# A decode step of two attention layers and two gated layers on one core: layer one's gated product, its turn and its products with w_down in two parts, in two PSUM banks, with another order of transfers

## The chip, the cores and the metric

The kernel runs on one core of one Trainium2 chip. The metric is the device time of one execution in microseconds; the figure for a kernel is the median of its runs. Three runs of the kernel before took 300.4, 301.22 and 302.75 us, so its time is 301.22 us. Lower is better.

## The reference, cut to what matters

```python
def _A_ref(x, k_cache, v_cache, wq, wo):        # x (4,1,512); caches (4,8,4096,128)
    q = (x @ wq).reshape(B, Sq, 32, 128).transpose(0, 2, 1, 3)
    k, v = repeat(k_cache, 4, axis=1), repeat(v_cache, 4, axis=1)
    p = softmax(einsum("bhqd,bhkd->bhqk", q, k) * 128 ** -0.5)
    o = einsum("bhqk,bhkd->bhqd", p, v)
    return o.transpose(0, 2, 1, 3).reshape(B, Sq, 4096) @ wo
def _B_ref(x, w_gate, w_up, w_down):            # 512 -> 1792 -> 512
    return (sigmoid(x @ w_gate) * (x @ w_up)) @ w_down
x = A_x
x = x + _A_ref(_layernorm(x), ...)              # attention, layer one
x = x + _B_ref(_layernorm(x), ...)              # gated layer, layer one
x = x + _A_ref(_layernorm(x), ...)              # attention, layer two: the same caches and weights
x = x + _B_ref(_layernorm(x), ...)
```

All arrays are bfloat16. The keys and the values of one sample are 8 heads of 4096 x 128 each, 8.4 MB; of four samples, keys and values together, 67 MB. Both attention layers read them, and a layer's result for a sample is needed before the next layer's query of that sample exists.

## The kernel before

**Units and tiles.** A unit is (sample b, half of the heads hg, layer l), written as three digits: 011 is sample 0, second half, layer two. There are sixteen; `UNITS` gives their order, and unit i of that order has the stages k{i}.0 and k{i}.1 (scores, L814), p{i} (softmax), v{i}.0 and v{i}.1 (products with the values, L942), o{i}.* (their sum turned and divided) and in layer one w{i}.* (products with wo, added to x). A tile is half of one head's keys or values, 128 x 2048 bfloat16, 0.52 MB. Keys are turned in place on VectorE before use (L824). The tiles of the second half of the heads (hg = 1) and one tile more stay in SBUF from layer one to layer two; those of the first half are loaded twice. So 114 MB are read.

**Transfers.** All of them are issued from SP's queue in the order of the string `LOADS`: `K2010` is the keys of unit 201, tiles 0 of a pair of heads, and makes two transfers of 0.52 MB; a last letter (`K201a`) makes one of 1.05 MB, both halves of a head. In this text transfers are numbered from 0 in this order; there are 156, in both kernels. A tile goes to a place in SBUF that the planner picks, and the issue waits until the last instruction that uses what was there is done. An issue that waits holds all behind it.

**Planner.** Every operation is put with a cost, a rank (with the shift that `SHIFTS` has for its stage) and what it reads and writes. `schedule` (L150) then plays the program through once, picks for each engine the operation that can start first (by rank among several), and so fixes the order on each engine, the places of the tiles, and fillers: matmuls on PE (L1329) with no use but to keep its clock up where it would idle. On the chip each engine runs its list in order.

**The chain of a sample.** When the last values of (b, 1, layer one) are in, `chain(b)` (L1127) runs: `layer_norm` (stage n), `gate_up` (g: 16 matmuls with w_gate into bank G, 16 with w_up into bank U, and on the way the norm's factor: PE, ACT, POOL), `gated` (h: tanh on ACT, L1092; product on VectorE, L1097; turn on VectorE, L1104), `down` (d: 56 matmuls with w_down, L1117, summed in bank G), the update of x (L1140), `layer_norm` again (m), and then the queries of layer two (q, L752). From then on the scores of unit (b, 1, 1) can be made, and the places that its kept keys hold come free. The chains of the four samples lie at about 87, 147, 198 and 253 us of the span. `gated` and `down` take a range of chunks of 128 rows of w_down (14 in all); the chain calls them once, with all 14. `last_chain` (L1212), the gated layer of layer two for all samples, calls `gated` in three parts already.

Of the kernel before, what the change touches and what calls it, by code (L numbers as in the profile page):

```python
# [7 lines left out]
ALU = mybir.AluOpType  # L8
# [31 lines left out]
class _Tile:  # L40
# [366 lines left out]
def bass_interleave_layers__gqa_block_cached__glu_gated_glu__decode_kernel(nc, A_x, A_k, A_v, A_wq, A_wo, B_x, B_wg, B_wu, B_wd, out):  # L407
    B, SQ, D = A_x.shape
    _, G, SK, DH = A_k.shape
# [4 lines left out]
    KD = D // P  # L414
# [7 lines left out]
    FB = FS // 32  # L422
# [6 lines left out]
    MORE = 64  # L429
# [3 lines left out]
    S = _Plan([SLOTS, 2, 2, 2, 2, 3, 3, 3, 8])  # L433
# [40 lines left out]
    q1 = sb("q1", [P, G, R, B], bf)  # L474
# [36 lines left out]
    G_ps = ps("G_ps", [P, 512])  # L511
    U_ps = ps("U_ps", [P, 512])
# [20 lines left out]
    def const(name, flat, first, parts):  # L533
# [15 lines left out]
        reads=["mask"], writes=["mask"], cost=0.3,  # L549
# [123 lines left out]
    def rank_v(u, pr):  # L673
# [9 lines left out]
        reads=["xin", "ident"], writes=[own("M", True)], cost=0.2, lock="M",  # L683
# [3 lines left out]
        reads=[own("M")], writes=[f"x{b}" for b in range(B)], cost=0.2, free="M",  # L687
# [391 lines left out]
    def gated(rs, rs_key, chunks, nb, rank, ends):  # L1079

        c0, c1 = chunks
        cols = slice(32 * c0, 32 * c1)
        share = (c1 - c0) / FB

        def dealt(t):
            return t[:, 0:FS].rearrange("p (i x) -> p i x", i=32)[:, :, c0:c1]

        def packed(t):
            return t[:, cols].rearrange("p (i x) -> p i x", i=32)

        S.put(
            "act", lambda e: e.activation(packed(th), dealt(G_ps), ACTF.Tanh, scale=rs),  # L1092
            reads=["G", rs_key] + [own("P") + "t0"] * (c0 > 0), writes=[own("P", c0 == 0) + f"t{c0}"], cost=0.18 + 0.47 * share, rank=rank, lock="P" if c0 == 0 else None,
        )
        S.put(
            "dve",
            lambda e: e.scalar_tensor_tensor(  # L1097
                out=packed(b1), in0=packed(th), scalar=1.0, in1=dealt(U_ps), op0=ALU.add, op1=ALU.mult,
            ),
            reads=[own("P") + f"t{c0}", "U"] + [own("B1") + "t0"] * (c0 > 0), writes=[own("B1", c0 == 0) + f"t{c0}"], cost=0.16 + 0.47 * share, rank=rank,  # L1100
            lock="B1" if c0 == 0 else None,
        )
        S.put(
            "dve", lambda e: e.transpose(  # L1104
                pt_h[:, cols].bitcast(dt.int32).rearrange("p (c i) -> p c i", i=32),
                b1[:, cols].bitcast(dt.int32).rearrange("p (i c) -> p c i", i=32),
            ),
            reads=[own("B1") + f"t{c0}"], writes=[own("P") + f"d{c0}"], cost=0.13 + 0.24 * share, rank=rank, free="B1" if c1 == FB else None,
        )

    def down(chunks, nb, o_ps, bank, rank):
        c0, c1 = chunks
        for k in range(KD):
            fns = []
            for c in range(c0, c1):
                rows = pt_h[:, 64 * (c // 2):64 * (c // 2) + 64].rearrange("p (i r) -> p i r", r=2)[:, 0:nb, c % 2]
                fns.append(lambda e, k=k, c=c, rows=rows: e.matmul(  # L1117
                    o_ps[:, k * MORE:(k + 1) * MORE], lhsT=wd[:, c, k * P:(k + 1) * P],
                    rhs=rows.unsqueeze(2).broadcast_to([P, nb, MORE // nb]),
                    start=(c == c0), stop=(c == c1 - 1),  # L1120
                ))
# [250 lines left out]
```

## Time and profile before

| | us |
|---|---|
| median of three runs | 301.22 |
| the profiled execution, whole | 301.75 |
| its span, first to last instruction | 300.0 |
| PE busy | 213.7 |
| VectorE (DVE) busy | 171.5 |
| ACT busy | 61.0 |
| share of the 16 DMA engines that q1's packets took | 94.8% |

The span has 1.75 us around it in this execution. A busy share is an average over the span; the engines wait for transfers at many places, and the transfers for places in SBUF at some. A row of the view by windows gives the busy time of each engine in a stretch, then the clock that PE was granted (1.00 is full), the share of the DMA engines in use and the rate of the transfers. In the chain of waits a row gives start, length, and the engine and line (or the transfer) that the end waited for at that time.

### The profile page before, as it was taken

Reading aid. Unit: us, or ns where it says so; the run is one execution under the profiler, and the core shown is the slowest. Engines: PE = TensorE matmul, PEld = TensorE weight load, DVE = VectorE, ACT = ScalarE, POOL = GpSimd, SP = SyncE. Lnnn points to the kernel's source line nnn. Section 1 sums busy time; section 2 is a strip of 40 time slices with the busy share of each in tenths; the row PEclk is TensorE's granted clock in tenths of the full one; section 3 lists DMA queues with packets and bytes.
Section 4 is the critical chain, followed back from the end, with each engine's and each line's share of the span. In section 5 each row is a group of like instructions: output and inputs, shape, how many; then the busy total and the mean of one; then the engine's idle time right before and its main releaser. Section 6 shows DMA issues by size and latency. Waiting matters only on the chain.

```text
span 300.0 us, 8879 instructions
## 1 busy us (share of the span) xinstructions
PE 213.7 (71%) x3977; PEld 129.4 (43%) x3977; DVE 171.5 (57%) x327; ACT 61.0 (20%) x155; POOL 13.0 (4%) x48
## 2 busy tenths in 40 slices
PE   1200205487888979688889878798886889898785
PEld 1200201134456637245456464456554355554462
DVE  4069593972004998956126986315997783258223
ACT  1100000123102210042323202322220233224212
POOL 8200000000000000000000000000000000000000
PEclk9999999559999999999999999999999799999999
DMA  6999999999999999999999999978999998999940
GB/s 263 384 412 413 419 411 424 414 422 417 401 416 407 376 415 419 417 417 412 407 407 354 406 413 413 411 304 352 354 416 423 417 407 323 398 401 417 416 178 4
DMA packets 25638, 114.62 MB, mean 382 GB/s; under 512 B 2560, under 2 KB 2560, under 8 KB 19840
## 3 DMA queue, kind: packets, MB, share of 16 engines
q1 hardware_dynamic: 25552, 114.04, 94.8%
q8 instruction: 31, 0.51, 0.7%
q14 instruction: 7, 0.06, 0.0%
q10 hardware_dynamic: 48, 0.01, 0.0%
HBM read 114.04 MB, written 0.00 MB: 380 GB/s over the span
## 4 chain that ended last, share of the span: by engine, by line
DMA 48%; PE 26%; SPq 14%; DVE 5%; issue 3%; ACT 2%; POOL 0%; DVEq 0%; ACTq 0%
DMA slots<-in_A_v_cache_dram 28%; DMA slots<-in_A_k_cache_dram 16%; SPq L603 13%; DMA wo<-in_A_wo_dram 5%; PE O_ps L962 4%; PE S_ps L832 4%; PE Q_ps L752 3%; PE M_ps L1003 3%; DVE slots L824 2%; PE G_ps L1117 2%; PE PT_ps L1329 2%; SPq L611 2%; PE M_ps L981 1%; ACT b L974 1%; PE G_ps L1065 1%
## 5 line engine op out<-in xcount | busy, mean ns | idle before, releaser
L824 DVE STREAM_TRANSPOSE slots<-slots 128x1024 int32<-128x1024 int32 x89 | 107.1, 1226 | 23.0 <-DMA slots<-in_A_k_cache_dram 21.5
L1329 PE MATMUL PT_ps<-even 128*128 128x256 bf16 x404 | 56.4, 273 | 0.8 <-ACT pt_sb L889 0.8
L832 PE MATMUL S_ps<-slots,qz 128*32 128x512 bf16 x488 | 39.7, 431 | 23.8 <-DVE slots L824 21.7
L962 PE MATMUL O_ps<-slots,pt_sb 128*16 128x512 bf16 x472 | 35.3, 381 | 12.5 <-DMA slots<-in_A_v_cache_dram 9.0
L1329 PEld LDWEIGHTS PT_ps<-even 128*128 128x128 bf16 x404 | 34.9, 99 | 15.8 <-issue 10.2
L974 ACT ACTIVATE b<-O_ps 128x512 bf16<-128x512 f32 x31 | 18.5, 595 | 59.8 <-PE O_ps L962 50.6
L832 PEld LDWEIGHTS S_ps<-slots,qz 128*32 128x32 bf16 x488 | 12.4, 100 | 41.2 <-DVE slots L824 25.3
L989 DVE TENSOR_TENSOR oT<-M_ps,rl 128x8 bf16<-128x8 f32 x31 | 4.7, 153 | 27.4 <-PE M_ps L981 27.4
L1003 PE MATMUL M_ps<-oT,wo 128*128 128x64 bf16 x512 | 19.0, 193 | 1.5 <-DVE x L1015 0.3
L962 PEld LDWEIGHTS O_ps<-slots,pt_sb 128*16 128x16 bf16 x472 | 9.6, 87 | 22.8 <-issue 7.1
L1003 PEld LDWEIGHTS M_ps<-oT,wo 128*128 128x128 bf16 x512 | 16.9, 98 | 6.0 <-DVE oT L989 2.4
L721 PE MATMUL Q_ps<-small,wq 128*128 128x4 bf16 x128 | 3.7, 166 | 21.3 <-DVE wsum L1306 18.8
L868 ACT ACTIVATE pp<-S_ps,tr 128x512 bf16<-128x512 f32 x16 | 13.3, 832 | 21.1 <-DVE tr L861 20.3
L981 PE MATMUL M_ps<-sel_o,b 128*64 128x64 bf16 x496 | 13.8, 199 | 4.4 <-ACT b L974 3.6
L981 PEld LDWEIGHTS M_ps<-sel_o,b 128*64 128x64 bf16 x496 | 10.4, 112 | 13.4 <-ACT b L974 10.5
L854 DVE TENSOR_REDUCE stat<-S_ps 128x1 f32<-128x512 f32 x16 | 10.9, 682 | 8.8 <-PE S_ps L832 8.7
L1055 POOL TENSOR_TENSOR stat<-stat 128x1 f32<-128x1 f32 x8 | 4.4, 551 | 251.5 <-ACT stat L1051 251.5
L889 ACT ACTIVATE pt_sb<-PT_ps 128x512 bf16<-128x512 f32 x16 | 9.5, 595 | 21.8 <-PE PT_ps L879 20.4
L801 DVE TENSOR_TENSOR qz<-Q_ps,maskrs 128x256 bf16<-128x256 f32 x16 | 6.5, 404 | 12.1 <-PE Q_ps L791 7.0
L721 PEld LDWEIGHTS Q_ps<-small,wq 128*128 128x128 bf16 x128 | 3.6, 104 | 21.5 <-DVE sq L1297 18.9
L796 ACT ACTIVATE maskrs<-mask,stat 128x16 f32<-128x16 f32 x16 | 4.5, 303 | 36.3 <-DVE qz L801 26.4
L1015 DVE SCALAR_TENSOR_TENSOR x<-M_ps,x 128x4 f32<-128x4 f32 x16 | 2.4, 148 | 12.6 <-PE M_ps L1003 12.4
(155 smaller groups left out, 205.1 us busy)
## 6 DMA issues: line engine op xcount, KB each, us to landing
slots<-in_A_v_cache_dram SPq DMA_DIRECT2D x51, 512.0 KB, 9.9
slots<-in_A_k_cache_dram SPq DMA_DIRECT2D x49, 512.0 KB, 7.7
slots<-in_A_k_cache_dram SPq DMA_DIRECT2D x20, 1024.0 KB, 13.1
slots<-in_A_v_cache_dram SPq DMA_DIRECT2D x19, 1024.0 KB, 13.7
wq<-in_A_wq_dram SPq DMA_DIRECT2D x2, 2048.0 KB, 15.0
wo<-in_A_wo_dram SPq DMA_DIRECT2D x4, 1024.0 KB, 13.6
wg<-in_B_w_gate_dram SPq DMA_DIRECT2D x1, 1792.0 KB, 26.5
wu<-in_B_w_up_dram SPq DMA_DIRECT2D x1, 1792.0 KB, 17.8
```

The lines of the kernel that those rows point to most:

```text
L603: return e.dma_start((ring if len(ts) == 1 else double)[ts[0].slot], src)
L752: fns.append(lambda e, c=c, k=k: e.matmul(Q_ps[:, c * WIDE:c * WIDE + MORE - c // 15 * WIDE], lhsT=wq[:, hg, k, c * DH:(c + 1) * DH], rhs= ...
L824: "dve", lambda e, t=t: e.transpose(ring[t.slot].bitcast(dt.int32), ring[t.slot].bitcast(dt.int32)),
L832: fns.append(lambda e, s=s, t=t, nn=nn, q=q: e.matmul(S_ps[qi][32 * s:32 * s + 32, :], lhsT=window(qi, s * NQ + nn, q), rhs=ring[t.slot].r ...
L854: dve(lambda e: e.tensor_reduce(ml[at], bank, AX.X, ALU.max, negate=True), keys(f"S{qi}", ss), keys("ml", ss), 0.7)
L868: lambda e: e.activation(p_sb[at].rearrange("p (t j r) -> p t r j", j=32, r=2), bank.rearrange("p (t r j) -> p t r j", r=2, j=32), ACTF.Ex ...
L889: "act", lambda e: e.activation(pt_sb[qi][:, cols], PT_ps[:, cols], ACTF.Copy),
L962: fns.append(lambda e, m=m, at=at, v=v, c=c, q=q: e.matmul(O_ps[m:m + 16, :], lhsT=pt[:, at:at + 16], rhs=ring[v.slot][:, c * 512:(c + 1) ...
L974: "act", lambda e: e.activation(b1[:], O_ps[:], ACTF.Copy),
L981: fns.append(lambda e, tt=tt, r=r, a=a: e.matmul(M_ps[64 * a:64 * a + 64, r * SP:(r + 1) * SP], lhsT=b1[:, bass.ds(tt * P + r, 64, step=2) ...
L1003: fns.append(lambda e, k=k, n=n, h0=h0: e.matmul(M_ps[:, k * MORE:(k + 1) * MORE], lhsT=wo[:, h0 + n, k * P:(k + 1) * P], rhs=oT[:, b, h0 ...
L1329: S.filler(lambda e: e.matmul(PT_ps[:, 0:256], lhsT=ident, rhs=flat_even[:, 0:256], start=True, stop=True), "PT")
```

## The change

`chain` calls `gated` twice, with chunks 0 to 5 and 6 to 13, so that tanh, product and turn come as two smaller instructions each; `down` is called for each part, the first with 24 matmuls into bank G, the second with 32 into bank U; and the update of x is made twice, first from G, then from U, the second with the sum over the row. `LOADS` is another order of the same transfers (the same number, and the same tiles as one and as two), and `SHIFTS` is another set of shifts, so that the orders on all engines and the places of the tiles are others too. Nothing else differs.

```diff
-SHIFTS = {"d0": 58.5, "d1": -16.5, "d2": -3.0, "d3": -16.0, "end": -8.5, "g0": -16.0, 
...
+SHIFTS = {"d0": 6.0, "d1": -4.5, "d3": 9.0, "end": 2.0, "g0": -8.0, "g1": 11.0, 
...
-LOADS = "wq0 wo3 wo2 K1000 K010d K000c wo1 wq1 K010a K000d K000b K010b K010c wg K000a K100d V000b K100c V000a K1002 V000d V000c V010c V010b V010a V010d wo0 wu wd V1000 V1001 K2000 K0013 K0011 K2003 K2001 K110c K2002 K110a K110b K110d V100c K0010 V100d V110a V110b K0012 V110c V110d V0010 V0011 V2002 V2003 V2000 V2001 K210c K3001 K2100 K3000 K3003 V0012 K2102 K210d V0013 K3002 V2100 V2101 V210d V210c V3002 V3003 V3000 K310a V3001 K1012 K1011 K2011 K1010 K3103 K1013 K3101 K310b K201b K201a V310b K2013 V310a V3102 V3103 V1012 V1013 V2012 V2013 K3011 V1010 V1011 K3013 K301b K301a V201a V301a V201b V301b V301C V301D"
+LOADS = "wq0 K100c K000d K000c wo3 K000a wo1 K000b K1000 K010a wo0 K010b K010c wo2 wq1 wu K010d K100d V000a K1002 V000d V000c V000b V010c V010a V010d V010b wg wd V1000 K110a V1001 K2001 K0010 K2000 K110c K110b K110d V100c V110c K0011 K0012 V100d K0013 K2002 K2003 V110a V110d V110b V2002 V2003 V2000 V2001 V0010 V0011 K2102 K3000 K2100 V0012 K210c K3001 K3003 K210d V0013 V210d K3002 V2100 V2101 V210c V3002 V3003 V3000 V3001 K1010 K1011 K3103 K1013 K310a K1012 K3101 K310b K201a K2011 K201b K2013 V310b V310a V3102 V3103 V1010 V1011 V1012 V1013 K3011 V2012 V2013 K3013 K301a K301b V201b V201a V301b V301a V301C V301D"
@@ chain
-        gated(rs, f"rsg{b}", (0, FB), 1, rank, True)
+        cuts = [(0, 6), (6, FB)]
+        for cut in cuts:
+            gated(rs, f"rsg{b}", cut, 1, rank, True)
         S.stage = f"d{b}"
-        down((0, FB), 1, G_ps, "G", rank)
-        S.put(
-            "dve",
-            lambda e: e.scalar_tensor_tensor(
-                out=x[:, b], in0=G_ps[:, bass.ds(0, KD, step=MORE)], scalar=rs, in1=x[:, b], op0=ALU.mult, op1=ALU.add,
-                accum_out=xsum[:, b:b + 1],
-            ),
-            reads=["G", f"rsg{b}", f"x{b}"], writes=[f"x{b}", f"xsum{b}"], cost=0.2, rank=rank,
-        )
+        for cut, o_ps, bank in zip(cuts, (G_ps, U_ps), "GU"):
+            down(cut, 1, o_ps, bank, rank)
+            more = dict(accum_out=xsum[:, b:b + 1]) if bank == "U" else {}
+            S.put(
+                "dve",
+                lambda e, o_ps=o_ps, more=more: e.scalar_tensor_tensor(
+                    out=x[:, b], in0=o_ps[:, bass.ds(0, KD, step=MORE)], scalar=rs, in1=x[:, b], op0=ALU.mult, op1=ALU.add, **more
+                ),
+                reads=[bank, f"rsg{b}", f"x{b}"], writes=[f"x{b}"] + [f"xsum{b}"] * (bank == "U"), cost=0.2, rank=rank,
+            )
```

What the new order is on the engines around sample 2's chain (stage, number of matmuls; fillers left out), as both kernels' instruction lists have it:

```
PE before: v8.1 16 | o8.1 16 | v9.1 4 | w8.1 32 | v9.1 4 | n2 | g2 4 | v9.1 8 | g2 norm | g2 12 | o9.1 16 | g2 16 | v9.0 8 | d2 56 | m2 | q10 32 | m2 norm | q10 32 | v9.0 8 | q10 4 | o9.0 16 | k10.0
PE after:  v8.1 16 | w8.0 24 | o8.1 16 | v9.1 8 | w8.1 32 | n2 | v9.1 4 | g2 12 | g2 norm | g2 20 | v9.1 4 | d2 56 | v9.0 8 | m2 | v9.0 8 | q10 32 | m2 norm | q10 32 | o9.1 16 | q10 4 | k10.0
DVE before: x (m2) | turn of two tiles of unit 310's keys | product for q10
DVE after:  x (m2) | turn of two tiles of unit 101's keys (transfers 105, 106) | product for q10
```

More of the change, by code (lines that the diff above doesn't have):

```diff
@@ L30 @@
 KEPT_V = 8.0
-SHIFTS = {"d0": 58.5, "d1": -16.5, "d2": -3.0, "d3": -16.0, "end": -8.5, "g0": -16.0, "g2": 10.5, "g3": -0.5, "h0": -3.0, "h1": -17.5, "h2": 2.5, "h3": 36.5, "k0.0": 12.5, "k0.1": 34.0, "k1.0": 0.5, "k1.1": -10.0, "k10.0": 6.0, "k10.1": 0.5, "k11.0": 5.0, "k11.1": 14.5, "k12.0": -2.5, "k12.1": -31.0, "k13.0": 12.0, "k13.1": 6.5, "k14.0": 25.0, "k14.1": 6.0, "k15.0": 30.5, "k15.1": -45.5, "k2.0": -11.0, "k2.1": -53.0, "k3.0": 6.0, "k3.1": 5.5, "k4.0": -1.5, "k4.1": 2.0, "k5.0": -36.5, "k5.1": 5.0, "k6.0": 134.5, "k6.1": 19.0, "k7.1": -9.0, "k8.0": 19.5, "k8.1": -4.0, "k9.0": 7.5, "k9.1": -2.5, "m1": -10.0, "m2": -2.0, "m3": 1.0, "mean0": -0.5, "mean1": 39.5, "n0": -23.5, "n1": -1.0, "n2": -17.5, "n3": 4.5, "o0.0": 9.5, "o0.1": -5.5, "o1.0": 3.0, "o10.0": 4.5, "o10.1": -16.0, "o11.0": -9.5, "o11.1": 10.0, "o12.0": 1.0, "o12.1": 9.0, "o13.0": 2.0, "o13.1": 3.0, "o14.1": 4.0, "o15.0": -1.0, "o2.0": 71.5, "o3.0": 21.0, "o4.0": 12.0, "o4.1": -5.0, "o5.0": -3.5, "o5.1": -41.0, "o6.0": -12.5, "o6.1": 4.5, "o7.0": -3.5, "o7.1": 5.0, "o8.0": -7.0, "o8.1": 3.0, "o9.0": -10.0, "o9.1": 8.5, "out": 8.5, "p0": -10.5, "p1": 2.0, "p10": -4.5, "p11": 11.5, "p12": 19.5, "p13": 21.5, "p14": 5.0, "p15": 46.5, "p2": 4.5, "p3": -0.5, "p4": -14.0, "p5": -2.0, "p6": -0.5, "p7": 5.0, "p8": -45.5, "p9": -3.5, "q0": -3.0, "q1": -26.0, "q10": 30.0, "q11": -11.0, "q12": 27.0, "q13": 5.0, "q14": -28.5, "q15": 41.5, "q2": -7.5, "q3": 25.5, "q4": 1.5, "q5": -4.0, "q6": -7.0, "q7": -19.0, "q8": 0.5, "q9": -2.0, "v0.0": -10.5, "v0.1": -20.0, "v1.0": -17.0, "v1.1": 7.0, "v10.0": -6.5, "v10.1": 17.0, "v11.0": 1.5, "v11.1": 10.0, "v12.0": 4.0, "v12.1": -4.5, "v13.0": 9.0, "v13.1": -28.0, "v14.1": -5.5, "v15.0": 24.0, "v15.2": -1.5, "v15.3": -35.0, "v2.0": 6.0, "v2.1": 3.0, "v3.0": -4.5, "v3.1": 17.5, "v4.0": -6.0, "v4.1": 8.5, "v5.0": -9.0, "v5.1": -4.5, "v6.0": -8.5, "v7.0": 0.5, "v7.1": 6.0, "v8.0": 0.5, "v8.1": 3.0, "v9.0": 10.0, "v9.1": -2.0, "w0.0": 4.0, "w0.1": -9.0, "w1.1": 6.0, "w11.0": -6.5, "w11.1": -13.0, "w2.0": 16.0, "w2.1": -4.0, "w4.0": 0.5, "w4.1": 11.5, "w5.0": -2.0, "w5.1": 2.0, "w8.0": -3.5, "w8.1": -12.0, "w9.0": 5.0, "w9.1": -16.5, "z0": 21.0, "z12": 22.5, "z16": 62.5, "z24": 9.5, "z8": 26.5}
@@ new lines @@
+SHIFTS = {"d0": 6.0, "d1": -4.5, "d3": 9.0, "end": 2.0, "g0": -8.0, "g1": 11.0, "g3": 26.0, "h2": 3.0, "h3": -7.5, "k0.0": 1.0, "k0.1": 10.0, "k1.1": 4.5, "k10.0": 1.0, "k10.1": 12.0, "k11.0": 2.5, "k11.1": 13.5, "k12.0": -9.5, "k12.1": 2.0, "k13.0": -102.5, "k13.1": 16.5, "k14.0": 2.5, "k14.1": 2.0, "k15.0": 5.0, "k15.1": 13.0, "k2.0": 6.0, "k2.1": -16.0, "k3.0": 13.5, "k4.0": -20.5, "k4.1": -7.0, "k5.0": 22.0, "k5.1": -29.5, "k6.0": 26.0, "k6.1": 4.0, "k7.0": 3.5, "k7.1": 8.5, "k8.0": 6.0, "k8.1": 37.5, "k9.0": 12.5, "k9.1": 5.0, "m0": 4.0, "m1": -4.5, "m2": -17.5, "m3": -55.0, "mean0": 3.0, "mean1": 14.0, "n0": -0.5, "n1": -7.0, "n2": 3.0, "n3": -26.5, "o0.0": -6.0, "o0.1": -8.0, "o1.0": -6.0, "o1.1": -5.0, "o11.0": 5.0, "o11.1": -11.0, "o12.0": -12.5, "o12.1": 0.5, "o13.1": 5.5, "o14.0": -6.0, "o14.1": -4.5, "o15.0": 10.5, "o2.0": 6.0, "o3.0": 14.5, "o3.1": 66.0, "o4.0": 31.0, "o5.0": 12.0, "o5.1": 3.0, "o6.0": 0.5, "o6.1": -4.0, "o7.0": -0.5, "o7.1": -11.5, "o8.0": 2.0, "o8.1": -5.5, "o9.0": 14.5, "o9.1": 17.0, "out": 10.0, "p0": -4.5, "p10": -18.5, "p11": 11.0, "p12": 60.0, "p13": 132.5, "p15": 12.5, "p2": 67.5, "p3": -4.5, "p4": 42.0, "p5": 53.0, "p6": 119.5, "p8": 2.5, "p9": 91.5, "q0": 7.0, "q1": -13.5, "q10": 0.5, "q11": -17.5, "q12": 6.0, "q13": 0.5, "q14": -11.5, "q15": -2.5, "q2": 6.0, "q3": 25.0, "q4": -13.0, "q5": -75.0, "q6": 1.5, "q7": 0.5, "q8": 12.0, "q9": -4.5, "v0.0": -3.0, "v0.1": 7.0, "v1.0": -12.5, "v1.1": 1.0, "v10.0": 10.5, "v10.1": 17.5, "v11.1": 1.5, "v12.0": -13.0, "v12.1": -31.0, "v13.0": -10.5, "v13.1": -9.5, "v14.0": 18.0, "v14.1": 8.5, "v15.0": -8.5, "v15.2": -23.5, "v15.3": -14.0, "v3.0": -49.5, "v3.1": -30.5, "v4.0": 27.0, "v5.0": 8.5, "v5.1": -42.0, "v6.0": -7.0, "v7.0": -34.5, "v7.1": 2.0, "v8.0": 2.5, "v8.1": -7.0, "v9.0": -9.0, "v9.1": 4.0, "w0.0": -2.5, "w0.1": -13.0, "w1.0": -10.5, "w1.1": 21.0, "w11.0": 126.0, "w11.1": -12.5, "w2.0": -15.5, "w2.1": -20.5, "w4.0": 4.5, "w4.1": -7.0, "w5.0": 22.0, "w5.1": 28.5, "w8.0": -4.5, "w8.1": 9.0, "z12": 8.5, "z16": -4.0, "z24": 2.0, "z8": 3.0}
```

## The prediction

> **What bounds the kernel now.** First the page: where the span goes by slices, and what its last chain waited for.
>
> ```profile
> PEclk9999999559999999999999999999999799999999
> DMA  6999999999999999999999999978999998999940
> GB/s 263 384 412 413 419 411 424 414 422 417 401 416 407 376 415 419 417 417 412 407 407 354 406 413 413 411 304 352 354 416 423 417 407 323 398 401 417 416 178 4
> ...
> DMA 48%; PE 26%; SPq 14%; DVE 5%; issue 3%; ACT 2%; POOL 0%; DVEq 0%; ACTq 0%
> ```
>
> The transfers run at 400 to 424 GB/s nearly throughout, so the stream bounds: 114 MB at 410 GB/s are 278 us, and the rest of the 300.0 is a start, a tail after the last landing, and holes. The view by windows sizes the holes (last column the rate):
>
> ```profile
> 96.00:106.00 10.00, 8.89 (x191) 6.53 (x191) 9.54 (x15) 3.38 (x11) 0.55 (x1) 1.00 1.00 384
> 156.00:168.00 12.00, 11.12 (x226) 7.69 (x225) 7.84 (x16) 3.73 (x13) 0.55 (x1) 1.00 0.98 371
> 198.00:202.00 4.00, 3.84 (x70) 1.91 (x70) 0.53 (x3) 1.85 (x6) 0.55 (x1) 1.00 0.56 200
> 208.00:216.00 8.00, 7.57 (x173) 4.77 (x170) 6.42 (x12) 3.02 (x9) 0.40 (x1) 1.00 0.82 306
> 247.00:254.00 7.00, 6.43 (x143) 3.82 (x144) 2.51 (x10) 1.57 (x5) 0.00 (x0) 1.00 0.89 320
> 287.00:300.00 13.00, 8.86 (x274) 6.29 (x274) 4.11 (x23) 2.25 (x9) 0.55 (x1) 0.95 0.11 41
> ```
>
> Missing bytes against 410 GB/s make 0.6, 1.1, 2.05, 2.05 and 1.55 us, 7.3 in all. Four lie in the chains of samples 0, 1, 2 (two); the fifth before sample 3's. The tail, from the last landing at 290.3 to the end, is 9.7. Only holes and tail can change: a faster chain is worth nothing unless a transfer waits for it.
>
> Why they open, from the chain of waits and SP's timeline round sample 2:
>
> ```profile
> 200.89 0.89 PE U_ps L1065 x16
> ...
> 201.87 0.63 DVE b L1097
> ...
> 202.53 0.59 DVE pp L1104
> ...
> 203.25 1.85 PE G_ps L1117 x56
> ...
> 207.57 0.98 PE Q_ps L752 x32
> 208.55 0.54 PE O_ps L962 x8
> ```
> ```profile
> 199.59 0.33 SPq L603 DMA_DIRECT2D slots<-in_A_k_cache_dram  x1
> ```
>
> Transfer 103 (K310a) took places that the last of v9.1 frees, and was issued at 199.59; 102 landed at 201.05. 108 waited for v9.0's second half, which stands behind the chain's q10, and was issued at 209.14; 107 landed at 210.79. Call **lead** the time from the end of an issue to the landing of the transfer before it: 1.13 and 1.32 us here, with holes of about 2. Leads of 2.7 to 3.1 (transfers 42, 77, 133) had the small ones; above 3.5 there was none. So I take hole = 3.3 less the lead. A 0.52 MB transfer is 1.27 us of stream.
>
> The Trainium skill (DMA: Bandwidth & Descriptors, Anatomy of one DMA) puts a transfer's fixed cost at about 2.0 us, so an estimated hole of 2.0 less the lead; the rows here have 2 us where that gives 0.9 and 0.7, so the trace does not agree.
>
> **Part by part: the chain.** Widths come from the view by form, the last chain having narrow ones:
>
> ```profile
> L1092 ACT ACTIVATE pp<-G_ps,stat 128x448 f32<-128x448 f32 x4 | 2.5, 633 | 2.3 <-PE G_ps L1065 0.8 <-PE M_ps L981 0.7 <-PE U_ps L1065 0.7
> L1092 ACT ACTIVATE pp<-G_ps,stat 128x192 f32<-128x192 f32 x2 | 0.8, 421 | 0.2 <-POOL stat L1234 0.2
> L1097 DVE SCALAR_TENSOR_TENSOR b<-pp,U_ps 128x192 bf16<-128x192 f32 x2 | 0.7, 334 | 0.5 <-PE S_ps L1258 0.5
> L1104 DVE STREAM_TRANSPOSE pp<-b 128x96 int32<-128x96 int32 x2 | 0.6, 305 | 0.0
> ```
>
> Removed: tanh 0.63, product 0.62, turn 0.58, 56 matmuls 1.85 (33 ns each); with gaps, factor to last matmul was 200.88 to 205.10, 4.22. Added: part one 0.42 + 0.33 + 0.31; part two, 256 wide, has no row and lies between those of 192 and 448: 0.47, 0.40, 0.37 by their slope. Tanh two runs beside product one. The path is 0.09 + 0.42 + 0.09 + 0.33 + 0.04 + 0.31, then on VectorE product and turn two with their gaps, 0.99 (24 matmuls, 0.79, lie beside), then 32 matmuls 1.05: 3.3, or 0.9 less per chain. Bounds: 1.3 less if part two costs as little as part one, 0.5 less at the cost of the full width. The update from G (0.22) lies beside the 32 matmuls; without that cover it costs 0.3. Bank U is read by product two before its matmuls can be ready, so it adds no wait.
>
> **The order.** I follow what releases each transfer in the new lists, with the durations above, and compare with the landing at the same byte. Without holes a landing depends on the bytes alone.
>
> - *Start and sample 0.* wo0 and wu come early, and w0.* is done before the last values; wg and wd land at 85.3 and 89.6 as wu and wd did. The layer norm starts some 0.9 earlier, but v2.0's second half now stands behind q3, and transfer 39 (K0010) waits for it at 39.2 MB, where before the first behind the chain was 42, at 40.3. Released near 97.9, lead 2.8: hole 0.5 (0 to 1.5), as before.
> - *Sample 1.* Two products with wo (1.15 each) come after the last o4, not one: the norm starts at about 148.2, not 147.0. The quicker chain and the statistic's matmul in mid-q7, not behind it, give it back; k7.0 starts at about 160.2 (160.3 before). But v6.0, on which 76 to 79 wait, is half in front of q7: leads 4.1, 3.5 and 3.8. Hole 0.5 (0 to 1.2) for 1.1.
> - *Sample 2.* K310a comes later, and 103 waits for v9.1's first half: lead 3.7, no hole. 105 needs its last four matmuls, now behind g2's 32: about 201.4, lead 1.85, hole 1.45. 107 needs v9.0's first half, behind d2: lead 2.35, hole 0.95. 111 needs k10.0, done at about 210.9 for 211.3: lead 2.4, hole 0.9. Sum 3.3 (1.5 to 6.5) for 4.1.
> - *Before sample 3.* 133 waited for k13.1, which had o11.0 and w11.0 (1.17) in its midst and its last turns behind p12 on VectorE, and was issued 4.5 after 126 landed. Now k13.1 follows v11.0 at once: about 246.6, lead near 4.8. Hole 0.2 (0 to 1) for 1.55.
> - *Sample 3.* Without that hole the stream is 1.3 ahead, and the chain's margin thinner: on ACT the copy of o12.0 (0.6) stands ahead of the factor's step. 145 waits for q14, near 263.8: lead 2.9, hole 0.4 (0 to 1.6) for 0.
> - *Tail.* Same last transfers, same code; four of z8's matmuls more lie ahead of the last values' second half: 0.2.
>
> Before 7.3; after 0.5 + 0.5 + 3.3 + 0.2 + 0.4 + 0.2 = 5.1: **2.2 us less**. On the profiled execution (span 300.0, 301.75 with what is around it) that is 299.5; it ran 0.5 above the median, so for the median 301.22 - 2.2 = **299.0**.
>
> **Rivals.**
>
> 1. *The holes close* (chance 0.13). If the worked leads suffice, 1 to 3 of the 5.1 stay: 301.2 - 7.3 + 1 to 3 = 294.9 to 296.9. For it: only 7.3 us in 300 are holes, and leads of 3.5 had none. Against: the two leads below 1.4 cost in full. By the skill's 2.0 only 105's hole would stay, of 0.15.
> 2. *The holes move* (0.16). A faster release lets the stream run ahead into the next chain, which then lacks margin, as with sample 3 here: 300.5 to 302. For it: leads of 3.5 to 4 are now many (76 to 80, 137 to 143). Against: after 202 and 216 the trace has full rate for 32 us.
> 3. *Slower: 105 is late* (0.22). On VectorE the turns of 105 and 106 (1.23 each) now stand ahead of q10's product; before, keys that had long landed stood there. If 105 lands after 206.4, the product is late by as much, and with it k10.0 and 111 to 117. Transfer 109 took 5.3 from issue to landing in such a place; 105 would then land at 207.0, and holes of 2.9, 1.0 and 2.9 make 6.8 for 3.3: 302.5, and up to 306 where samples 1 and 3 lose as well (their bounds, 0.7 and 1.2, and 1.5 from the holes at 107 and 133). Against: 108 took 2.9, hence 205.1.
> 4. *Slower: the parts do not overlap* (0.06). Each instruction has a fixed part: widths 64, 192 and 448 give 0.31, 0.42, 0.63 on ACT, so 0.25; on VectorE 0.15 and 0.10. In series the chain is 0.5 longer, not 0.9 shorter: 1.4 later at each release, four holes larger by it: 304.6. Against: in the last chain's parts ACT starts at 295.30 and VectorE at 295.40, side by side. The Trainium skill (VectorE: DVE Perf Modes, The TRN2 errata) warns of just that, a fixed extra per instruction that narrow tiles pay each time; the widths agree.
>
> **How the numbers follow.** The forecast, 297.5 to 300.5, has 0.43. Bounds of about 1%, what a measurement of this kernel can tell from no change, are 298.2 and 304.2. Faster: rival 1 and a quarter of the forecast, 0.24; slower: half of rival 3, and rival 4, 0.17; within, 0.59. The range 296.2 to 304.4 leaves out some 0.07 of rival 1, 0.08 of rival 3 and most of rival 4, 0.2 in all.
>
> **What would show it.** Right: L1092, L1097 and L1104 in two widths, with about 3.3 us from the factor to the last L1117; no hole at 199 and none at 248; a rate of 306 or more where v9 and k10.0 lie. Wrong: SP waiting for k10.0 past 211.5 with VectorE at L824 just ahead of L801 (rival 3); 4.7 us for that path (rival 4); a new dip before 265 at sample 3 (rival 2); the tail over 10 us.

## The result and the profile after

The kernel after takes 299.38 us (median of 13 runs, 298.22 to 301.29) beside 301.38 for the kernel before (13 runs on the same chip): a ratio of 0.9922, 95% interval 0.9897 to 0.9946. The forecast was 299.0, or 2.2 us less; it is 2.0 less. Two further sets of runs of the same kernel, below, gave 0.9956 (0.9921 to 0.9991) and 0.9918 (0.9883 to 0.9953), so 1.3 and 2.5 us less. The profiled execution took 299.44, its span is 297.7 for 300.0.

The page of the kernel after, slices and the shares of the chain that ended last:

```profile
PEclk9999955599999999999999999999999999999979
DMA  7999999999999999999999999998999999999930
GB/s 259 429 387 422 407 401 413 415 422 418 412 417 411 368 420 416 413 416 413 409 388 389 363 419 411 415 405 307 382 409 420 418 408 407 403 403 424 409 149 3
...
DMA 49%; PE 24%; SPq 18%; DVE 5%; issue 3%; ACT 1%; DVEq 0%
```

The stream still bounds. Of the three slices of before at 304, 352 and 354 GB/s (195 to 217 us) one is left, 307 (with 382 behind it), and the one at 323 near 250 is gone; the dip of sample 1 (354 before) is one of three slices, 388, 389 and 363. The view by windows of the kernel after (last column the rate), in the stretches shown of before:

```profile
96.00:106.00 10.00, 9.06 (x167) 5.43 (x167) 8.80 (x16) 3.55 (x9) 0.02 (x1) 1.00 1.00 381
156.00:168.00 12.00, 9.41 (x185) 6.90 (x185) 8.22 (x13) 3.23 (x11) 0.55 (x1) 1.00 1.01 370
198.00:202.00 4.00, 3.54 (x61) 1.91 (x58) 0.41 (x3) 1.16 (x5) 0.55 (x1) 1.00 0.96 381
208.00:216.00 8.00, 7.56 (x174) 4.82 (x173) 6.78 (x14) 3.52 (x10) 0.20 (x1) 1.00 1.00 377
247.00:254.00 7.00, 5.88 (x120) 3.38 (x119) 1.31 (x7) 2.83 (x9) 0.00 (x0) 1.00 1.03 408
```

Against 410 GB/s these miss 0.7, 1.2, 0.3, 0.65 and 0.0 us; between 202 and 208 some more, so that 198 to 218 misses 2.6 in all (its row stands with one_part_2 below). The same stretch of the kernel before missed 4.05:

```profile
198.00:218.00 20.00, 17.44 (x380) 11.52 (x384) 12.34 (x24) 6.20 (x20) 1.10 (x2) 1.00 0.85 327
```

The hole at 199 (2.05 before) and the one at 248 (1.55) are gone, those of samples 0 and 1 are not.

The groups by form of the kernel after show the two widths:

```profile
L1092 ACT ACTIVATE pp<-G_ps,stat 128x192 f32<-128x192 f32 x6 | 2.5, 420 | 3.7 <-PE U_ps L1065 1.4 <-DMA wd<-in_B_w_down_dram 1.3 <-PE M_ps L981 0.7
...
L1092 ACT ACTIVATE pp<-G_ps,stat 128x256 f32<-128x256 f32 x4 | 1.9, 474 | 0.1
...
L1104 DVE STREAM_TRANSPOSE pp<-b 128x128 int32<-128x128 int32 x4 | 1.6, 405 | 0.1
L1097 DVE SCALAR_TENSOR_TENSOR b<-pp,U_ps 128x256 bf16<-128x256 f32 x4 | 1.5, 380 | 0.0
```

Part two costs 0.474, 0.380 and 0.405 us, for 0.47, 0.40 and 0.37 estimated. The chain of waits of the kernel after at sample 2:

```profile
201.55 0.43 ACT pp L1092
...
202.00 0.37 DVE b L1097
...
202.39 0.32 DVE pp L1104
...
202.84 0.88 PE G_ps L1117 x24
203.72 0.96 PE U_ps L1117 x32
204.68 0.54 PE O_ps L962 x8
```

Only part one's three steps are on the path; part two's lie beside the 24 matmuls into G, and PE then runs all 56 without a gap. The forecast had part two's product and turn (0.99) on the path, with the 24 matmuls beside them; it is the other way round, at nearly the same length (0.88). From the factor (201.45) to the last matmul (204.68) it is 3.23 us, for 4.22 before and 3.3 forecast.

### The profile page after: what moved, and what is told of

Same layout as the page of the kernel before. It is cut to its first block, busy times and chain, and to the rows that moved or that the text cites. A ratio compares the mean times of both kernels' runs of the same rounds, so it can differ in the third digit from the quotient of the medians.

```text
span 297.7 us, 8902 instructions
## 1 busy us (share of the span) xinstructions
PE 212.8 (71%) x3981; PEld 130.8 (44%) x3981; DVE 173.0 (58%) x339; ACT 62.0 (21%) x159; POOL 13.0 (4%) x48
## 4 chain that ended last, share of the span: by engine, by line
DMA 49%; PE 24%; SPq 18%; DVE 5%; issue 3%; ACT 1%; DVEq 0%
DMA slots<-in_A_v_cache_dram 37%; SPq L603 14%; DMA slots<-in_A_k_cache_dram 12%; PE O_ps L962 5%; SPq L611 4%; PE S_ps L832 4%; PE M_ps L1003 3%; DVE slots L824 2%; PE Q_ps L752 2%; PE M_ps L981 1%; PE G_ps L1065 1%; PE U_ps L1117 1%; PE PT_ps L1332 1%; PE U_ps L1065 1%; PE G_ps L1117 1%
## 5 line engine op out<-in xcount | busy, mean ns | idle before, releaser
L832 PE MATMUL S_ps<-slots,qz 128*32 128x512 bf16 x488 | 37.8, 423 | 30.3 <-DVE slots L824 27.1
L1332 PEld LDWEIGHTS PT_ps<-even 128*128 128x128 bf16 x408 | 35.9, 99 | 15.9 <-issue 8.9
L832 PEld LDWEIGHTS S_ps<-slots,qz 128*32 128x32 bf16 x488 | 12.6, 100 | 46.5 <-DVE slots L824 29.5
L1003 PE MATMUL M_ps<-oT,wo 128*128 128x64 bf16 x512 | 19.8, 193 | 3.0 <-issue 1.9
L874 DVE STREAM_TRANSPOSE pp<-pp 128x256 int32<-128x256 int32 x16 | 6.8, 425 | 5.2 <-ACT pp L868 5.2
```

Of the source, the lines that this page charges most:

```text
L832: fns.append(lambda e, s=s, t=t, nn=nn, q=q: e.matmul(S_ps[qi][32 * s:32 * s + 32, :], lhsT=window(qi, s * NQ + nn, q), rhs=ring[t.slot].r ...
L1003: fns.append(lambda e, k=k, n=n, h0=h0: e.matmul(M_ps[:, k * MORE:(k + 1) * MORE], lhsT=wo[:, h0 + n, k * P:(k + 1) * P], rhs=oT[:, b, h0 ...
L1332: S.filler(lambda e: e.matmul(PT_ps[:, 0:256], lhsT=ident, rhs=flat_even[:, 0:256], start=True, stop=True), "PT")
```

## The experiments

All kernels below compute the whole reference. Each was run beside the kernel before on one chip, and the ratio is to it. The last columns are worked out from the landings in each profile: the time between two amounts of bytes landed, less those bytes at 410 GB/s. Sample 0 is 36 to 62 MB, sample 1 62 to 80, sample 2 80 to 97, sample 3 97 to 113.5. A profile is one execution, and such a column moves by some 0.5 from one to the next; for sample 1 it moved from 1.4 to 3.3 between three profiles of the kernel after. A transfer is called late by the time from the landing before it to its own, less its bytes at 410 GB/s.

| kernel | median us | ratio, 95% interval | missing at sample 0, 1, 2, 3 (us) |
|---|---|---|---|
| before | 301.38 to 302.1 | 1 | 0.5, 1.0, 4.7, 1.5 |
| after | 299.38 | 0.9922 (0.9897 to 0.9946) | 0.5, 1.8, 2.0, 1.0 |
| after_again | 300.1 | 0.9956 (0.9921 to 0.9991) | 0.8, 1.4, 2.4, 0.9 |
| after_third | 299.18 | 0.9918 (0.9883 to 0.9953) | 0.6, 3.3, 2.3, 0.9 |
| split_only | 304.19 | 1.0043 (1.0012 to 1.0074) | 0.7, 4.0, 3.3, 2.3 |
| split_v5_first | 301.56 | 0.9987 (0.9947 to 1.0028) | 0.5, 0.9, 4.0, 1.0 |
| one_part | 301.65 | 0.9984 (0.9949 to 1.0019) | 1.1, 0.6, 3.9, 1.2 |
| one_part_01 | 300.38 | 0.9951 (0.9920 to 0.9983) | 0.4, 1.5, 2.4, 0.9 |
| one_part_23 | 301.47 | 1.0009 (0.9979 to 1.0040) | 0.9, 0.7, 4.0, 1.4 |
| one_part_2 | 301.48 | 0.9982 (0.9948 to 1.0015) | 0.6, 0.8, 4.1, 1.2 |
| one_part_3 | 299.52 | 0.9943 (0.9905 to 0.9982) | 0.4, 1.6, 3.0, 0.7 |
| w5_behind_k7 | 299.4 | 0.9906 (0.9871 to 0.9941) | 0.5, 1.4, 3.0, 0.9 |
| v91_ahead_g2 | 299.64 | 0.9893 (0.9844 to 0.9941) | 0.6, 0.7, 3.3, 1.6 |
| three_moves | 298.92 | 0.9894 (0.9858 to 0.9929) | 0.7, 0.8, 2.7, 0.5 |

**Each half alone: split_only and one_part.** The first is the change to `chain` without the two lists:

```diff
-        gated(rs, f"rsg{b}", (0, FB), 1, rank, True)
+        cuts = [(0, 6), (6, FB)]
+        for cut in cuts:
+            gated(rs, f"rsg{b}", cut, 1, rank, True)
...
```

> The chain in two parts, with the order of transfers and work of the kernel before. Times beside 301.4 for before and 299.4 for after. Theory A (each part of the change pays for itself: a faster chain lifts every transfer that waits behind it): the chain of each sample 0.9 shorter; the transfers behind it (42 at sample 0, 77 at sample 1, 108 at sample 2) are released 0.5 to 0.9 earlier, and the holes that belong to the order (103 at 199 us, 133 at 248 us) stay at 2 and 1.5: 299.0 to 300.0. Theory B (the order brings it all, the chain's gain is swallowed by the next chain): 301.4. Theory C (the chain brings it all, the order nothing): 299.4, with the holes at 199 and 248 gone or worth nothing.

The second is the kernel after with the order on every engine kept as it is, part one's tanh, product and turn widened to all 14 chunks, and part two's three instructions dropped after the plan is made:

```diff
-            gated(rs, f"rsg{b}", cut, 1, rank, True)
+            gated(rs, f"rsg{b}", cut, 1, rank, True, whole=cut[0] == 0)
...
+        for b in range(4):
+            for e in ("act", "dve"):
+                parts = [op for op in self.prog[e] if op.stage == f"h{b}"]
+                half = len(parts) // 2
+                for one, two in zip(parts[:half], parts[half:]):
+                    self.prog[e].remove(two)
```

> The order of the kernel after, instruction for instruction, but tanh, product and turn of each chain in one pass of the full width, as before; only the sum stays in two banks. Theory A: factor to last product with w_down 4.1 to 4.3 us for 3.23, so 39 (sample 0), 80 (sample 1) and 107 and 111 (sample 2) are released 0.9 later, and each of three stretches loses 0.5 to 1.0: 301.0 to 302.2. Theory B (the order brings it all): 299.4. By the sum of the prediction with one row changed, 3.3 back to 4.2, each hole grows by what its lead loses.

Neither half shows a gain by itself: 1.0043 and 0.9984, where the two together make 0.992 to 0.996. All three theories missed split_only: it is slower. SP's timeline of split_only shows where:

```profile
149.68 0.33 SPq L603 DMA_DIRECT2D slots<-in_A_v_cache_dram  x1
154.12 9.31 SPq L603 DMA_DIRECT2D slots<-in_A_k_cache_dram  x9
```

Transfer 73 was issued at 154.12, where before it was 152.25. It waits for v5.1's second half. The plan plays the program through with the costs, found the chain of sample 1 ready earlier, and put v5.1's last four matmuls behind d1's 56 (before: all eight ahead of d1), and v5.0's first eight behind q7. The stream lost 2.7 us there (62 to 66 MB). So "the order of before" was not what ran, and the next kernel puts these two steps back (a few other steps on PE stay moved, none of them round sample 2's chain).

**split_v5_first.** split_only with two steps moved on PE after the plan is made (the numbers are the operations' own):

```diff
+        pe = self.prog["pe"]
+        for ns, ahead in [([593], 532), ([578, 579], 542)]:
+            part = [op for op in pe if op.n in ns]
+            pe[:] = [op for op in pe if op.n not in ns]
+            at = [op.n for op in pe].index(ahead)
+            pe[at:at] = part
```

> The kernel with the chain in two parts in the order of before (1.0043 of before), with two steps put back to where the kernel before has them on TensorE: v5.1's last four matmuls ahead of d1's and not behind, v5.0's first eight ahead of m1 and not behind q7. There 73 was issued at 154.1 for 152.2 and 75 at 158.5 for 155.6, and the stream lost 2.8 us on the kernel before. If these two steps are why the chain in two parts did not pay in the old order: 73 near 152.2, 75 near 155.0, and the time 299.5 to 301 at 301.4 for before (0.993 to 0.999). If the faster chain is worth nothing in the old order: 1.000. If something else made it slow: 1.004 again.

Transfer 73 went out at 151.9, the loss at sample 1 is 0.9 again, and the ratio fell by 0.0056 to 0.9987. So these two steps made split_only slow; its stream shows it, while the two intervals still overlap by 0.0016. The ratio lies at the edge of what the first theory gave and its interval holds 1.000: a faster chain in the old order is worth little or nothing. SP's timeline of split_v5_first says why:

```profile
199.20 0.33 SPq L609 DMA_DIRECT2D slots<-in_A_k_cache_dram  x1
199.57 1.07 SPq L609 DMA_DIRECT2D slots<-in_A_v_cache_dram  x2
201.84 12.28 SPq L609 DMA_DIRECT2D slots<-in_A_k_cache_dram  x10
```

103 (K310a) is released at 199.20 by v9.1's last matmuls, ahead of the chain, at a lead of 1.12 for 1.13 before. This hole no faster chain can touch. The second hole of sample 2 is smaller by 0.4 (208 to 216 us at 325 GB/s, for 306 before), and sample 2 misses 4.0 in all, for 4.7 before.

**Which chain pays: one_part_01, one_part_23, one_part_2, one_part_3.** The edit of one_part, for some samples alone:

```diff
+            gated(rs, f"rsg{b}", cut, 1, rank, True, whole=cut[0] == 0 and b in (0, 1))
...
+        for b in (0, 1):
```

> The kernel after with tanh, product and turn in one pass of the full width in the chains of samples 0 and 1 alone. One pass in all four chains cost 0.6% of the time (0.9984 of before, for 0.9922). If holes add up (the prediction's sum): 0.9 at sample 0 and up to 0.9 at sample 1, so 0.9 to 1.8 us over after. If what is lost ahead of sample 2 is made up there (there the path from the last landing of v8's values to the release by k10.0 sets the stream, and it starts later only by what the landing is later): 0 to 0.5 over after.

> The same in the chains of samples 2 and 3 alone. If holes add up: 0.9 at sample 2 (107 and then 111 later) and 0.5 to 0.9 at sample 3 (145 waits for q14, at a lead of 3.3), so 1.4 to 1.8 us over after, about as much as samples 0 and 1 together. If the last chains set the end and the first are covered: 1.5 to 2.0 over after, the whole cost of one pass in all four.

> The kernel after with tanh, product and turn in one pass of the full width in the chain of sample 2 alone. Samples 2 and 3 together cost 0.53% (1.6 us) over after. If sample 2's chain pays: 0.9 to 1.6 over after, with 1 us or more of it missing between 80 and 90 MB. If sample 3's chain takes back what the stream loses ahead of it, as sample 2 does for sample 1: 0 to 0.3.

> The same in the chain of sample 3 alone. In the kernel after nothing is missing there (leads of 3.1 to 3.4 at 143 and 145), so by the rule hole = 3.3 less the lead a chain longer by 0.9 opens 0.6 to 0.9: 0.6 to 0.9 over after. If the chain of sample 3 has slack: 0 to 0.2.

Beside the kernel after on the same chip: samples 0 and 1 cost nothing that can be told (0.9951 for 0.9956; the intervals leave room for about 1 us), samples 2 and 3 0.53% or 1.6 us, sample 2 alone 0.64% or 1.9 us (0.9982 for 0.9918, the intervals overlap by 0.0005), sample 3 alone 0.25%, within its interval. So the four chains do not pay alike: samples 2 and 3 together pay more than samples 0 and 1 (1.0009 for 0.9951, the intervals overlap by 0.0004), and sample 2's chain is the one whose cost shows by itself. Small costs of the others are not excluded: with its chain in one pass sample 3 had 143 late by 0.56 at a lead of 2.47, near the 0.6 to 0.9 of the rule. Sample 2's windows, first the kernel after, then one_part_2:

```profile
198.00:218.00 20.00, 18.46 (x388) 11.85 (x386) 13.36 (x29) 7.08 (x22) 1.10 (x2) 1.00 0.96 357
```
```profile
198.00:218.00 20.00, 17.89 (x371) 11.15 (x371) 11.99 (x23) 6.81 (x21) 1.10 (x2) 1.00 0.87 318
```

At 410 GB/s 2.6 and 4.5 us are missing, 1.9 more. That it equals the difference of the medians is chance in part: these two executions differ by 1.0 (299.44 and 300.48), since the kernel after missed 1.0 more at sample 1. The chain of waits of one_part_2:

```profile
200.76 0.64 ACT pp L1105
...
201.43 0.63 DVE b L1110
...
202.08 0.59 DVE pp L1117
...
202.80 0.88 PE G_ps L1130 x24
203.68 0.96 PE U_ps L1130 x32
```

Three full widths make the path from the tanh's start to the last matmul 3.88 us, where the kernel after has 3.13 (201.55 to 204.68): 0.75 longer. Behind it 107 (places of v9.0's first half) goes out at a lead of 0.58, for 1.2 to 1.6 in the three profiles of the kernel after, and 107 and 108 together land 2.1 late for 1.2 to 1.4. At 111 the lead was 2.65 and 1.0 late, for 0.2 to 0.8. The 0.75 of chain costs 1.9 of time by the ratios, and their intervals leave about 0.5 to 3.4; so that it costs more than its own length is not shown, and if it does, these runs do not say why.

**Idle time at sample 1: after_again, after_third, w5_behind_k7.** PE's timeline of the kernel after has a row that no step of the forecast had:

```profile
158.54 0.84 PE L1003 MATMUL M_ps<-oT,wo 128*128 128x64 bf16 x22
161.25 0.23 PE L1003 MATMUL M_ps<-oT,wo 128*128 128x64 bf16 x2 [1.86 <-issue]
161.41 2.04 PE L832 MATMUL S_ps<-slots,qz 128*32 128x512 bf16 x32
```

PE stood still for 1.86 us in the midst of w5.0, waiting for nothing that the profile names, and k7.0 (L832), whose keys' places transfer 80 needs, began at 161.4 although its query was ready at 159.2. The kernel after was run again unchanged, twice, and once with these matmuls behind k7.1:

```diff
+        for ns, ahead in [([585, 586, 587], 588)]:
...
```

> The kernel after, unchanged, for a second profile and beside the next three on one chip. If the 1.86 us in which TensorE stood idle among w5.0's matmuls belongs to the kernel, it is there again, k7.0 starts near 161.6 and transfer 80 is issued near 162.5. If it belongs to that one execution, k7.0 starts near 159.8 and 80 is issued near 160.8, and the stream is 1 us ahead of the first profile at 70 MB; the time is the same, 0.992 of before, if later stretches take that back.

> The kernel after, unchanged, so that the next three stand beside it on the same chip: 0.992 to 0.996 of before. Against 410 GB/s it missed 2.05 and 1.05 us between 62 and 70 MB (sample 1) and 2.21 and 2.56 between 80 and 90 MB (sample 2) in the first two profiles, 4.3 and 3.6 together. If what sample 1 loses is made up at sample 2: 3.5 to 4.5 together again, whatever the share of each.

> The kernel after with one step moved on TensorE: the first three groups (24 matmuls, L1003) of w5.0 stand behind k7.1's last, not ahead of k7.0's first. In the kernel after TensorE stood idle for 1.86 us among these matmuls (159.38 to 161.25 us), waiting for nothing that the profile shows, and k7.0 and transfer 80 came that much later; the hole there measures 1.2. If the idle time belongs to these matmuls: k7.0 starts near 159.5, 80 is issued near 160.8, the hole closes to 0.1, and the time is 298.3 (1.1 less than after). If it belongs to the place in the sequence of instructions (so many of them in a dense row), it falls into k7.0 instead, 80 is issued as late, and the time is 299.4. If later holes swallow it: 80 is early, and the time still 299.4.

It is not a single accident: at the same matmul it was 1.59 us in after_again, 3.23 in after_third, 1.32 in one_part_23 and in one_part_3. Nor does it always come: there was none in v91_ahead_g2, one_part_2, one_part and one_part_01, whose PE lists are the same up to there. With the matmuls moved, the first row of k7.0 in w5_behind_k7 names the query's product on VectorE as what it waited for:

```profile
159.08 0.26 PE L797 MATMUL Q_ps<-small,even 128*128 128x16 bf16 x4
159.92 2.25 PE L838 MATMUL S_ps<-slots,qz 128*32 128x512 bf16 x32 [0.59 <-DVE qz L807]
```

k7.0 starts 1.6 earlier than in after_again and the stream is 0.95 us ahead of the first profile at 68 MB; but at 92 MB nothing of that is left, and the time is that of the kernel after, within some 1.5 us by the intervals. These profiles suggest that what sample 1 wins, sample 2 gives back: where sample 1 missed 0.7 to 1.8 us, samples 1 and 2 together missed 3.5 to 4.6 in after, after_again, one_part_01, one_part_3, w5_behind_k7, v91_ahead_g2 and three_moves. The longest halt was not made up: 5.6 in after_third, whose profiled execution took 301.01 us. With one profile of each kernel, and steps at sample 2 moved in two of them, this is a trend and not shown.

**v91_ahead_g2 and three_moves.** v9.1's last four matmuls go ahead of g2; in three_moves also w5.0 as above and o12.0's sum behind g3.

```diff
+        for ns, ahead in [([827], 749)]:
...
+        for ns, ahead in [([585, 586, 587], 588), ([827], 749), ([1008], 1010)]:
```

> The kernel after with v9.1's last four matmuls, which free the places of transfers 105 and 106, ahead of g2's 32 and not behind them: 105 is released near 199.8 for 201.9, at a lead of 4.1 for 1.95, and the chain of sample 2 is 0.4 longer. By the rule of the prediction (hole = 3.3 less the lead) 105's hole of 1.35 goes: 298.3 to 298.6. By the landings of the kernel after (105 landed 1.38 behind 104, where the bytes alone take 1.27) there is no hole to win there, and the 0.4 on the chain moves 107 and 111: 299.4 to 299.9.

> The kernel after with three groups moved on TensorE: w5.0's first 24 matmuls behind k7.1 (sample 1), v9.1's last four ahead of g2 (sample 2), o12.0's 16 (0.38 us, in the midst of g3's) behind g3, into the wait for the tanh (sample 3). If holes add up: 1.1, 0.1 and up to 0.4 less, 298.0. If sample 2 takes back what sample 1 wins, and the chain's own length is all that counts: 0.4 longer at sample 2 and 0.4 shorter at sample 3, the time of after within 0.5.

105 went out at 198.9 with a lead of 3.99 and no hole, but 107 at a lead of 0.98, and 107 and 108 landed 2.4 late for 1.2 to 1.4: the hole moved on by two transfers. three_moves has the lowest median (298.92, and 298.09 to 299.74 over its six runs) and the shortest span, 296.5. Its interval overlaps that of the kernel after on the same chip, so a gain over it is not shown.

## Why the prediction was right, and where only its sum was

- **The bound, and the chain.** Right: the stream bounds, and factor to last matmul takes 3.23 us for 3.3, with part two's three steps within 0.04 of their estimates; which of the two stood on the path, part two on VectorE or the 24 matmuls, was taken the wrong way round, which made 0.1 of difference. The update from G (0.221) lies beside U's matmuls. Rival 4 (no overlap, 4.7 us) is out.
- **The holes at 199 and before sample 3.** Right: 103 has a lead of 3.98 (3.7 forecast); 133 was issued at 244.08, 2.5 earlier than forecast, and nothing is missing there.
- **Sample 2.** The forecast was 3.3 for 4.1; the stretch from 198 to 218 misses 2.6 by its window. 105, 107 and 111 were issued at 201.93, 205.27 and 210.65, within 0.5 of the forecast, with leads of 1.95, 1.23 and 2.34. Mis-sized was the rule "hole = 3.3 less the lead": it gives 1.35 at 105, where 0.1 was missing (0.2 and 0.5 in the two other profiles); at 107 and 108 it gives 2.1, 1.8 and 1.7 for 1.4, 1.3 and 1.2 measured; at 111 1.0, 0.8 and 0.8 for 0.7, 0.8 and 0.2. The fixed 2.0 us of the Trainium skill (DMA: Bandwidth & Descriptors, Anatomy of one DMA), stated there for transfers that GpSimd issues while these are issued by SP, gives 0.05 at 105, where the trace agrees, and 0.8 and none at 107 and 111, where it does not. No one line fits all three places. The reading behind the rule was loose as well: it set leads of 2.7 to 3.1 beside holes in windows, and found none above 3.5. By the landings of the kernel before, 42 and 133 (leads 2.77 and 2.72) were on time, and 1.37, 1.22 and 1.19 were lost at 43, 106 and 138, at leads of 3.54, 4.49 and 4.3: the loss came one to five transfers behind the one that was issued late.
- **Sample 0.** 39 was issued at 97.79 (97.9 forecast) at a lead of 2.65; the window misses 0.7 for 0.5, before 0.6.
- **Sample 1.** The forecast was 0.5 for 1.1; measured 1.8, 1.4 and 3.3 by the landings. One step that failed is "k7.0 starts at about 160.2": PE halted among w5.0's matmuls and it started at 161.4 to 163.2. The leads of 76 to 79, 4.1 to 5.6, were no shorter than forecast, and yet 76 was late by 0.68, where the rule has no hole. So the halt is not the whole of it: sample 1 missed 0.7 to 3.3 in the five profiles with a halt of over 1 us, and 0.6 to 1.5 in the six without one that have the new order.
- **Sample 3.** 145's hole of 0.4 did not come (lead 3.31, nothing missing). Of the 0.9 to 1.0 that sample 3 misses, 0.8 or more lies behind 106 MB, among the last transfers, which are issued far ahead; no term had it (before missed 0.1 there, and the other kernels in the new order between -0.3 and 0.8). The tail grew by 0.26, from 9.71 to 9.97, for 0.2; but by the last landing it was 9.45 and 9.80 in after_again and after_third, for 9.75 before, so a growth is not shown.
- **The sum.** That holes add up is the step that held least. One pass in the first two chains has no cost that can be told, and the profiles suggest that what sample 1 loses, up to about 2 us, comes back at sample 2; if so, the terms of samples 0 and 1 had no place in a sum. Two errors stood against each other in the first profile's windows, 0.7 too little at sample 1 (1.2) and 0.7 too much at sample 2 (2.6), and the total of 2.2 came out at 2.0. That it came so close is luck in part.
- **Why both halves are needed.** The forecast counted the new order and the shorter chain as separate gains. The runs have no gain for either alone that can be told from none, and 0.4 to 0.8% for both. The order without the shorter chain is clearly short of both together (one_part, 0.9949 to 1.0019, for 0.9897 to 0.9946). The shorter chain without the order is so beside the mean of the three sets of the kernel after (split_v5_first, 0.9947 to 1.0028, for 0.993), but not beside the one set on its own chip (0.9921 to 0.9991). The reason is read from the issues: in the old order a release ahead of the chain opens the first hole at sample 2; in the new one the chain's own releases (107, 111) do, and there its length counts. No run moved 103 alone in the old order.
- **The other rivals.** Rival 3: 105 landed at 205.59, and VectorE was done with 106's turn at 208.15, before q10's product started (209.02; its wait was for ACT, L796). Rival 1, 294.9 to 296.9, is out: 5.3 us are still missing by the landings. Rival 2, that holes move, did not come in the kernel after as put, at sample 3, but it is what the stream did with both further gains, in w5_behind_k7 and v91_ahead_g2.

## What to carry to other kernels

Where a stream is held up at several places, do not add the places up: lengthen one chain at a time and see which one the time follows; here one chain of four had a cost that could be told from none. When a planner decides the order, an edit that "leaves the order alone" may not: freeze the lists, and move single steps, or the experiment measures the plan. A release that a shorter chain cannot reach can hide most of its gain, so look for what holds the first late transfer before shortening what comes behind it.

## What the runs showed of the hardware

**PE halted behind a late load of instructions.** The page of the kernel after lists a queue of instruction loads:

```profile
q1 hardware_dynamic: 25552, 114.04, 95.8%
q8 instruction: 31, 0.51, 0.7%
```

By the trace's records of packets, q8 carries 16,384 bytes at a time; the profile does not name the engine that it serves. Ahead of the end of each halt one of these packets came in, and PE went on 1.3 to 1.5 us after it:

| kernel | q8's packet, from and to | PE goes on | halt |
|---|---|---|---|
| after | 158.98 to 159.94 | 161.25 | 1.86 |
| after_again | 159.12 to 160.08 | 161.40 | 1.59 |
| after_third | 160.73 to 161.72 | 162.99 | 3.23 |
| one_part_23 | 158.44 to 159.50 | 160.95 | 1.32 |
| one_part_3 | 158.21 to 159.16 | 160.63 | 1.32 |
| v91_ahead_g2 | 155.61 to 156.70 | | none |
| one_part_2 | 156.45 to 157.44 | | none |
| one_part | 156.92 to 158.00 | | none |
| one_part_01 | 157.68 to 158.64 | | none |

The latest packet goes with the longest halt, and where it came at 155.6 to 157.7 there was none. When this packet started, PE had begun 323 to 375 of its recorded instructions since the packet before where it then halted, and 212 to 254 in the four without a halt. w5_behind_k7 and three_moves had late packets too (159.13, 158.99) but the long score matmuls at this point in place of short ones: w5_behind_k7 had no halt, and three_moves one of 0.22 in the midst of k7.0, to 161.38, 1.41 after its packet's end. The Trainium skill (Runtime: NRT & Kernel Launch, Instruction fetch mechanics) says that an engine's instructions are refilled in blocks of 16 KiB over a DMA queue of its sequencer, and that this is mostly hidden; the packets' size agrees, and if the packet is the cause, it is not hidden here, in a dense run of matmuls of 38 ns beside a full stream. That the late packet is the cause is read from these times and not shown; no run changed the packet alone, and what made it late in some executions is open.

**A transfer's hole does not follow from its lead alone.** At a lead of 1.9 to 2.1 transfer 105 lost 0.0 to 0.5 us in nine profiles; 108 lost 1.0 to 2.5 at 1.8 to 2.1 in one_part, one_part_2, one_part_23, v91_ahead_g2 and three_moves, behind a 107 that was late itself. And single transfers with leads of 5 to 17 land 0.3 to 1.7 late, in the kernel before too, mostly at other places in each execution (75 of after_third: lead 5.2, 1.7 late). What makes them late is open.
